# Products with v and logits in 32-column tiles, the bits of a pair moved beside them

## The chip, the cores and the metric

The kernel runs on one core of a Trainium2 chip. The metric is the device time of one execution, in microseconds (us). The engines are PE (matrix products; its weight loads have rows of their own, PEld), DVE (vector), ACT (activations and copies), POOL (elementwise here), and SP, which issues nearly all DMAs.

## What is computed

Thirty-two attention heads (4 batches of 8, sequence 768, head size 64) in which a query sees only keys of its own hash bucket, then a soft mixture of experts over the result:

```python
q_bits = (np.einsum('bhsd,dk->bhsk', q, proj) > 0)        # k_bits alike
mask = q_bucket[:, :, :, None] == k_bucket[:, :, None, :]
scores = np.where(mask, scale * q @ k.T, -1e9)
attn = np.exp(scores - scores.max(-1)); attn /= attn.sum(-1) + 1e-9
x = (attn @ v) as [3072, 512]
logits = x @ phi                     # 32 slots
slot_input = softmax(logits, 0).T @ x
slot_out = relu(slot_input[e] @ w1[e]) @ w2[e]   # 8 experts
out = softmax(logits, 1) @ slot_out
```

## The kernel before

Heads go in pairs; a pair shares one load of q and k (`raw`, two tiles of 384 KB, one buffer each). Every step is a small function (`bits`, `smax`, `scores`, `exps`, `av`, `pair_sum` and so on). The order of the program is written out by hand: each step gets a place, a number in slots (a head has 6 slots, a pair 12), from the tables `WHEN` (relative to the head's or the pair's start, repeated for all), `FIRST` (first heads) and `LAST` (last heads); `at` collects the steps, `plan.sort` orders them, and each engine executes its own instructions in that order. So a place says what stands before what on an engine, not a time.

Per head, `smax` forms masked products (128-wide tiles, stationary operand 128 columns wide) of which DVE takes row maxima (`most`), `shift` and `shift_rows` put these into the operands, `scores` forms the final products in PSUM tiles `st` (3 buffers), ACT takes the exponentials (`exps`, into `pt`), POOL adds them up (`acc`), and `av` multiplies them with v: for each of 6 key blocks, two products with a stationary operand of 64 columns, one into partitions 0 to 63 of a PSUM tile and one into 64 to 127. Six such steps stand close together. The even head's six stand at 12m + 7.3 to 7.8 (m numbers the pairs), the odd head's at 12m + 11.4 to 11.9.

Per pair, `pair_sum` adds the columns of `acc` with a stationary operand of 32 columns in four tiles side by side, `pair_log` forms the logits with a 64-column operand in two tiles, `pair_rec`, `pair_add`, `pair_turn` and `pair_x` normalise and transpose. `bits` forms the hash projections of a pair with a 32-column operand in four tiles, and DVE turns them into signed bits at once (`over`, into `bt`, one buffer), from which `spread_bits` moves rows into the operands of both heads by DMA. The sums and logits of pair m stand beside the even head's products of pair m + 1; the bits of pair m + 2 stand alone at 12m + 9.77, among 128-wide products. `split_hi` (two ACT casts) and `split_lo` (DVE) split `raw`.

The PSUM pool `p_mi` (tiles `mi`, two buffers) serves, in turn, the sums, the logits, `shift`, the bits, `pair_turn` and `pair_x`. Products of plain fp32 stand in the trace as two records for each call, that is two passes over the moving operand.

The expert weights are 64 pieces of 512 KB. 22 buffers (`wa`) are filled while attention runs, 5 more (`wb`) at slot 178, when the pool `pp` (raw, w4, bt) is freed, the others as further pools are freed; the experts' products (lines 1250 and 1304, operands of 32 columns in four tiles) end the kernel.

Of the kernel before, what the change touches and what calls it, by code (L numbers as in the profile page):

```python
# [35 lines left out]
N_WA, N_WB, N_WX, N_WY, N_WP, N_WL, N_WQ, N_WC = 22, 5, 3, 3, 4, 4, 3, 1  # L36
# [9 lines left out]
WHEN = {'load': -22.2619,  # L46
 'bits': -14.2349,
 'split_hi': -13.1979,
 'split_lo': [-12.6935, -11.1565],
 'spread': [[-13.1488, -10.4354, -5.4444, -6.6523], [-12.5668, -12.3196, -12.1201, -12.1119]],  # L50
 'load_v': [-3.3718, -2.7975],
 'smax': [[-9.1416, -8.9962, -8.5159, -6.9351, -7.288, -7.9448, -7.6967, -6.8281, -5.1392, -5.8132, -5.3072, -5.9654], [-9.427, -9.0393, -8.9496, -8.0893, -6.5956, -5.4862, -5.2511, -6.7187, -5.9555, -4.4901, -4.4112, -4.8313]],
 'scores': [[1.2975, 4.5102, 4.6485, 0.1975, 0.9854, 3.1771, 3.9797, 1.6303, 4.9362, 3.6592, 4.7491, 2.6803], [0.1022, 0.1134, 0.2578, -0.7876, 2.5023, -0.0474, -0.0019, 0.9469, 3.5414, 3.836, 4.3557, 2.1267]],
 'shift': [-3.9548, -2.943],
 'shift_rows': [-3.1833, -2.5735],
 'acc': [[5.8167, 7.9352, 8.671, 8.9926, 9.4278], [3.2448, 5.9632, 7.775, 7.9389, 9.119]],
 'av': [[7.3359, 7.3407, 7.3716, 7.6009, 7.6538, 7.8216], [5.4279, 5.6255, 5.6962, 5.7798, 5.8356, 5.8843]],
 'pair_sum': 19.3148,
 'pair_turn': 22.5366,
 'pair_rec': [19.5377, 20.5566, 20.2507],  # L60
 'pair_log': 20.0405,
 'pair_x': [22.7561, 23.3606],
 'pair_add': 20.646,
 'batch_both': 22.6105,
 'batch_max': 23.0026,
 'batch_exp': 24.3365,
 'batch_turn': 28.9128,
 'batch_scale': 25.2342,
 'batch_slots': 31.0753,
 'batch_weigh': 30.6347,  # L70
 'batch_share': 31.0459,
 'batch_arrange': 31.5634,
 'load_weights': 19.2952,
 'most': [[-8.9336, -8.4993, -6.5106, -7.0012, -7.2304, -6.107, -4.4997, -4.045, -5.7193], [-9.2445, -8.5848, -7.9972, -6.5189, -4.7861, -6.6917, -4.8511, -3.3259, -3.4925]],
 'exps': [[2.4996, 4.6616, 1.3422, 1.7274, 4.1008, 2.657, 5.6835, 5.3516, 2.8997], [0.4665, 0.6159, -0.1385, 3.5659, 1.9029, 1.0907, 3.8797, 4.6698, 2.4268]]}

FIRST = {('bits', 0): -79.2532,
 ('first_x', 0): -21.5961,
 ('first_x', 1): -38.3467,
 ('first_x', 2): -14.0186,  # L80
 ('first_x', 3): -18.1728,
 ('load', 4, 0): -11.7737,
 ('load', 4, 1): -2.4487,
 ('bits', 2): -14.1697,
 ('split_hi', 2): -6.2964,
 ('split_lo', 2, 0): -6.0272,
 ('split_lo', 2, 1): -2.7126,
 ('spread_y', 2): -1.2972,
 ('spread_bits', 2): -10.7536,
 ('spread_l', 2): -0.8689,  # L90
 ('spread_x', 2): 1.8345,
 ('smax', 1, 0, 0): -15.417,
 ('smax', 1, 0, 1): -10.3075,
 ('smax', 1, 1, 0): -8.5553,
 ('smax', 1, 1, 1): -13.1999,
 ('smax', 1, 2, 0): -7.7817,
 ('smax', 1, 2, 1): -3.054,
 ('smax', 1, 3, 0): -2.9369,
 ('smax', 1, 3, 1): -6.0953,
# [3 lines left out]
 ('smax', 1, 5, 1): -12.1189,  # L103
 ('first_y', 1): -50.9549,
# [4 lines left out]
 ('bits_rest',): -35.6422,  # L109
 ('bits_copy', 0): -76.9767,  # L110
 ('bits_copy', 1): -74.0135,
 ('first_w', 0, 0): -52.4417,
 ('first_w', 0, 1): -39.9607,
 ('copy_ident',): -29.6374,
 ('bits_out',): -11.9627,
 ('shift_first', 0): -19.0897,
 ('rows_first', 0): -18.172,
# [5 lines left out]
 ('most', 1, 4): -3.6817,  # L123
# [4 lines left out]
 ('most', 1, 11): -11.3295,  # L128
 ('bits_first', 1): -42.9165,
 ('split_hi', 0): -76.3743,  # L130
 ('split_lo', 0, 0): -31.1399,
 ('split_lo', 0, 1): -29.5113,
 ('spread_x', 0): -28.9558,
 ('load_v', 0): -17.5538,
 ('smax', 0, 0, 0): -47.8465,
 ('scores', 0, 0, 0): -13.1602,
 ('most', 0, 0): -31.4902,
 ('exps', 0, 0): -9.5739,
 ('smax', 0, 0, 1): -30.0548,
 ('scores', 0, 0, 1): -8.5463,  # L140
 ('smax', 0, 1, 0): -28.1934,
# [3 lines left out]
 ('smax', 0, 1, 1): -53.0109,  # L145
 ('scores', 0, 1, 1): -7.7493,
 ('most', 0, 3): -42.0509,
 ('exps', 0, 3): -6.5603,
 ('smax', 0, 2, 0): -37.8114,
 ('scores', 0, 2, 0): -10.6797,  # L150
 ('most', 0, 4): -30.2579,
 ('exps', 0, 4): -9.0316,
 ('smax', 0, 2, 1): -23.4528,
 ('scores', 0, 2, 1): -3.1498,
 ('smax', 0, 3, 0): -23.0743,
 ('scores', 0, 3, 0): -2.8625,
 ('most', 0, 6): -22.0438,
 ('exps', 0, 6): 1.1398,
 ('smax', 0, 3, 1): -25.2842,
 ('scores', 0, 3, 1): -0.4211,  # L160
 ('most', 0, 7): -23.2425,
 ('exps', 0, 7): 2.139,
 ('smax', 0, 4, 0): -17.1968,
 ('scores', 0, 4, 0): -11.14,
 ('most', 0, 8): -16.3427,
 ('exps', 0, 8): -8.0057,
 ('smax', 0, 4, 1): -21.9959,
 ('scores', 0, 4, 1): -5.8002,
# [82 lines left out]
 ('exps', 2, 6): 13.8394,
 ('smax', 2, 3, 1): 4.3584,
# [180 lines left out]
def lsh_attention_soft_moe(  # L433
# [956 lines left out]
```

## Time and profile before

| | us |
|---|---|
| median of 3 runs | 479.09 |
| lowest, highest | 478.86, 481.44 |
| the profiled execution | 479.32 |
| its span (first to last instruction) | 477.4 |
| PE busy | 465.7 (98%) |
| DVE, POOL, ACT busy | 356.8, 334.0, 272.7 |

The mean granted clock of PE was 0.995 of full speed. Start times in a timeline are exact to 0.01 us; the end of a matrix product is modelled and overlaps the next start, so prices are taken from start to start.

### The profile page before, as it was taken

How to read it: one execution, taken by the hardware profiler on the slowest of the kernel's cores; microseconds unless marked ns; L12 is line 12 of the kernel's file. 1: busy time of each engine (PE TensorE's matmuls, PEld its weight loads, DVE VectorE, ACT ScalarE, POOL GpSimd, SP SyncE). 2: the span in 40 equal slices, each digit the busy share in tenths (PEclk: the TensorE clock that was granted, in tenths of full speed). 3: DMA queues.
4: the chain of work that ended last, by engine and by line, in shares of the span. 5: the costliest groups of instructions: out<-in, count | busy, mean ns of one | idle time of the engine just before them, and what ended most of it. 6: DMA issues, size and time to landing. Idle time of an engine off the chain costs nothing.

```text
span 477.4 us, 9268 instructions
## 1 busy us (share of the span) xinstructions
PE 465.7 (98%) x3337; PEld 297.7 (62%) x3337; DVE 356.8 (75%) x657; ACT 272.7 (57%) x515; POOL 334.0 (70%) x207
## 2 busy tenths in 40 slices
PE   8999999999999999999999999999999999999993
PEld 6764657575757565657566575757575666663682
DVE  5867787879788797979797878787888965464142
ACT  5666566575767564756575665657575654423232
POOL 8489796969686799696947999696767997810000
PEclk9999999999999999999999999999999999999998
DMA  5774555757575747576665657675755176899986
GB/s 170 179 164 120 134 130 134 220 147 209 156 200 144 202 121 185 167 173 195 151 217 132 188 137 215 153 210 155 199 147 127 40 169 243 345 409 395 411 342 266
DMA packets 37664, 93.09 MB, mean 195 GB/s; under 512 B 7074, under 2 KB 13348, under 8 KB 37620
## 3 DMA queue, kind: packets, MB, share of 16 engines
q1 hardware_dynamic: 37492, 92.37, 66.4%
q8 instruction: 26, 0.43, 0.4%
q14 instruction: 18, 0.15, 0.1%
q10 hardware_dynamic: 96, 0.07, 0.1%
q0 software_dynamic: 32, 0.07, 0.0%
HBM read 52.76 MB, written 6.29 MB: 124 GB/s over the span
## 4 chain that ended last, share of the span: by engine, by line
PE 93%; DMA 3%; DVE 2%; SPq 0%; issue 0%; ACT 0%; DVEq 0%; ACTq 0%
PE st L754 29%; PE av L780 26%; PE smx L691 15%; PE qs L1304 3%; PE qh L1250 3%; PE mi L641 3%; PE mi L792 2%; PE mi L805 2%; PE mi L840 2%; DMA w<-w 2%; PE mi L825 1%; PE av L550 1%; PE mi L739 1%; DMA raw<-qk 1%; PE mi L998 1%; PE qh L1327 1%
## 5 line engine op out<-in xcount | busy, mean ns | idle before, releaser
L771 POOL TENSOR_TENSOR acc<-acc,pt 128x768 f32<-128x768 f32 x125 | 243.7, 1951 | 11.8 <-ACT pt L760 4.7
L760 ACT ACTIVATE pt<-st 128x512 f32<-128x512 f32 x288 | 164.6, 596 | 60.1 <-PE st L754 56.3
L754 PE MATMUL st<-XY 128*128 128x512 f32 (+1 forms) x768 | 179.1, 343 | 0.0
L703 DVE TENSOR_REDUCE mx<-smx 128x1 f32<-128x512 f32 x192 | 130.5, 687 | 32.1 <-PE smx L691 30.7
L754 PEld LDWEIGHTS st<-XY 128*128 128x128 f32 x768 | 124.2, 189 | 31.4 <-issue 18.3
L780 PE MATMUL av<-pt,v 128*64 128x384 f32 x768 | 132.6, 491 | 0.0
L691 PE MATMUL smx<-XY 96*128 96x256 f32 (+1 forms) x384 | 119.0, 363 | 1.5 <-DVE mx L703 1.0
L780 PEld LDWEIGHTS av<-pt,v 128*64 128x64 f32 x768 | 51.7, 136 | 69.3 <-issue 64.5
L768 POOL TENSOR_TENSOR acc<-pt 128x768 f32<-128x768 f32 x32 | 58.7, 1834 | 41.1 <-ACT pt L760 40.9
L691 PEld LDWEIGHTS smx<-XY 96*128 96x128 f32 x384 | 68.9, 190 | 26.3 <-DVE mx L703 10.7
L700 DVE TENSOR_REDUCE mx<-smx 128x2 f32<-128x512 f32 x96 | 65.2, 679 | 1.9 <-PE smx L691 0.9
L784 ACT COPY avs<-av 128x384 f32<-128x384 f32 x32 | 15.3, 479 | 83.6 <-PE av L780 83.6
L799 DVE RECIPROCAL sm<-sm 128x128 f32<-128x128 f32 x45 | 40.5, 929 | 15.6 <-ACT sm L795 15.5
L598 DVE TENSOR_TENSOR w<-raw,w 128x768 fp32r<-128x768 f32 x28 | 37.4, 1337 | 0.9 <-ACT w L594 0.5
L594 ACT CAST w<-raw 128x768 fp32r<-128x768 f32 x30 | 23.4, 829 | 0.7 <-DMA XY<-mr 0.3
L611 ACT CAST XY<-w 64x768 fp32r<-64x768 f32 x30 | 23.4, 829 | 0.0
L842 DVE TENSOR_TENSOR xq<-mi,r 128x256 f32<-128x256 f32 x45 | 17.5, 417 | 5.9 <-PE mi L840 5.5
L1304 PE MATMUL qs<-w 128*32 128x128 f32 x464 | 15.4, 274 | 0.3 <-issue 0.3
L1304 PEld LDWEIGHTS qs<-w 128*32 128x32 f32 x464 | 13.9, 110 | 2.0 <-issue 1.9
L840 PE MATMUL mi<-ident,avs 128*128 128x128 f32 x90 | 14.8, 273 | 0.0
L641 PE MATMUL mi<-raw,pb 128*32 128x384 f32 x120 | 13.8, 502 | 0.8 <-DMA raw<-qk 0.8
L1250 PE MATMUL qh<-w,siT 128*32 128x512 f32 x128 | 14.4, 594 | 0.0
(191 smaller groups left out, 325.6 us busy)
## 6 DMA issues: line engine op xcount, KB each, us to landing
w<-w SPq DMA_DIRECT2D x61, 512.0 KB
XY<-w SPq DMA_DIRECT2D x47, 384.0 KB
XY<-w SPq DMA_DIRECT2D x63, 192.0 KB
raw<-qk SPq DMA_DIRECT2D x30, 384.0 KB
v<-vt SPq DMA_DIRECT2D x32, 192.0 KB
out<-w SPq DMA_DIRECT2D x9, 512.0 KB
xq<-w SPq DMA_DIRECT2D x3, 512.0 KB
out<-w SPq DMA_DIRECT2D x6, 256.0 KB
```

Of the source, the lines that this page charges most:

```text
L598: (nc.vector if h > 2 else nc.gpsimd).tensor_tensor(out=w[:, 2 * x + 1], in0=st[h]["raw", x], in1=w[:, 2 * x], op=ALU.subtract)
L691: nc.tensor.matmul(pt[:, o:o + b - a], s["Y"][0:96, 0, t * P:(t + 1) * P], s["Y"][0:96, 1, a:b], start=True, stop=True)
L700: nc.vector.tensor_reduce(out=mx[:, n - 1:n + 1], in_=s["sm_ps", n - 1].rearrange("p (a x) -> p a x", a=2), axis=AX.X, op=ALU.max)
L703: nc.vector.reduce_max(out=mx[:, n:n + 1], in_=s["sm_ps", n], axis=AX.X)
L754: nc.tensor.matmul(pt[:, o:o + b - a], x[:, 1, i * P:(i + 1) * P], x[:, 0, a:b], start=first, stop=not first)
L760: nc.scalar.activation(s["P", n // 4][:, 512 * u:512 * u + 512], s["st_ps", n - (n % 4 == 2)], AF.Exp, scale=D ** -0.5)
L768: nc.gpsimd.tensor_tensor(out=s["acc"], in0=pr[:, 0:S], in1=pr[:, S:2 * S], op=ALU.add)
L771: eng.tensor_tensor(out=s["acc"], in0=s["acc"], in1=pr[:, a * S:(a + 1) * S], op=ALU.add)
L780: nc.tensor.matmul(s["av"][64 * c:64 * c + 64, 0:HC], s["v"][:, i, :], pr[:, o + c * HC:o + (c + 1) * HC], start=(i == 0), stop=(i == NT - 1))
L799: nc.vector.reciprocal(out=rs[:, k * P:(k + 1) * P], in_=rs[:, k * P:(k + 1) * P])
L1250: nc.tensor.matmul(ph[fh][32 * j:32 * j + 32], siT[:, k, 4 * g + j, :], wt[0, g, k, j][:, fh * 512:(fh + 1) * 512], start=(k == 0), stop=( ...
L1304: nc.tensor.matmul(pos[i][32 * j:32 * j + 32, 0:w], hTs[g][:, f, 32 * j:32 * j + 32], wt[1, x, 2 * g + f // 4, j][:, (f % 4) * HM + o:(f % ...
```

## The change

- `av` makes four products with 32-column operands in place of two with 64, into the same PSUM rows; `pair_log` likewise.
- The bits of pair m + 2 move from 12m + 9.77 to 12m + 7.08, in front of the even head's products with v; their sign step becomes a step of its own (`bits_over`, at 12m + 7.40), and `bt` gets two buffers.
- `wa` has 21 buffers and `wb` 6; the tile `halves` of the last stage is taken from `wb` instead of `wa`.
- All places are set anew.

```diff
-N_WA, N_WB, N_WX, N_WY, N_WP, N_WL, N_WQ, N_WC = 22, 5, 3, 3, 4, 4, 3, 1
+N_WA, N_WB, N_WX, N_WY, N_WP, N_WL, N_WQ, N_WC = 21, 6, 3, 3, 4, 4, 3, 1
...
- 'bits': -14.2349,
+ 'bits': -16.9197,
+ 'bits_over': -16.6042,
...
- 'av': [[7.3359, 7.3407, 7.3716, 7.6009, 7.6538, 7.8216], [5.4279, 5.6255, 5.6962, 5.7798, 5.8356, 5.8843]],
+ 'av': [[7.1625, 7.3716, 7.5845, 7.6308, 7.8325, 7.9673], [5.4369, 5.5215, 5.7534, 5.7926, 5.8443, 5.9134]],
  'pair_sum': 19.3148,
...
- 'pair_log': 20.0405,
+ 'pair_log': 19.6449,
...
@@ bits
-        bt = pts[3][:, 2 * P:2 * P + HC].bitcast(F32R) if h == 0 else pp.tile([P, HC], F32R, name="bt", bufs=1)
+        bt = pts[3][:, 2 * P:2 * P + HC].bitcast(F32R) if h == 0 else pp.tile([P, HC], F32R, name="bt", bufs=2)
...
         else:
-            over(bt, pts_b[0], slice(0, P))
+            st[h]["pj"] = pts_b[0]
+
+    def bits_over(h):
+        over(st[h]["bt"], st[h]["pj"], slice(0, P))
@@ av
         for c in range(2):
-            nc.tensor.matmul(s["av"][64 * c:64 * c + 64, 0:HC], s["v"][:, i, :],
-                             pr[:, o + c * HC:o + (c + 1) * HC], start=(i == 0), stop=(i == NT - 1))
+            for e in range(0, D, 32):
+                nc.tensor.matmul(s["av"][64 * c + e:64 * c + e + 32, 0:HC], s["v"][:, i, e:e + 32],
+                                 pr[:, o + c * HC:o + (c + 1) * HC], start=(i == 0), stop=(i == NT - 1))
@@ pair_log
         for a in range(2):
-            nc.tensor.matmul(pt[64 * a:64 * a + 64, 0:HC], phs[:, 2 * g + a].rearrange("p c s -> p (c s)"),
-                             st[h + a]["avs"], start=True, stop=True)
+            for c in range(2):
+                r = 64 * a + 32 * c
+                nc.tensor.matmul(pt[r:r + 32, 0:HC], phs[:, 2 * g + a, c], st[h + a]["avs"], start=True, stop=True)
@@ the plan
             at(s0 + WHEN["bits"], bits, h)
+            if h > 2:
+                at(s0 + WHEN["bits_over"], bits_over, h)
...
-    halves = piece().bitcast(F32R)
+    halves = wb.tile([P, F], F32, name="w").bitcast(F32R)
```

Sorted by the new places, the even head's stretch of a pair reads on PE: bits of pair m + 2, `av` 0, sums of pair m - 1, `av` 1 to 3, logits of pair m - 1, `av` 4 and 5. After it stand 15 steps of 128-wide tiles, then the odd head's six `av`, then 38 steps of 128-wide tiles.

## Rows read from the trace of the kernel before

**Rows 1.** The page, part 1: busy time of each engine, share, instructions.

```profile
PE 465.7 (98%) x3337; PEld 297.7 (62%) x3337; DVE 356.8 (75%) x657; ACT 272.7 (57%) x515; POOL 334.0 (70%) x207
```

**Rows 2.** The page, part 4: the chain that ended last, by engine.

```profile
PE 93%; DMA 3%; DVE 2%; SPq 0%; issue 0%; ACT 0%; DVEq 0%; ACTq 0%
```

**Rows 3.** Groups by form, PE: line, tiles, stationary and moving shape, count, busy us.

```profile
L780 PE MATMUL av<-pt,v 128*64 128x384 f32 x768 | 132.6, 491 | 0.0
L792 PE MATMUL mi<-acc,ones 128*32 128x384 f32 x120 | 12.7, 496 | 0.0
```

**Rows 4.** Timeline of PE, 206 to 232 us: start, length, instruction, count.

```profile
206.39 0.85 PE L792 MATMUL mi<-acc,ones 128*32 128x384 f32 x8
207.18 4.09 PE L780 MATMUL av<-pt,v 128*64 128x384 f32 x24
211.09 0.82 PE L805 MATMUL mi<-avs,phs 128*64 128x384 f32 x4
211.84 1.19 PE L754 MATMUL st<-XY 128*128 128x512 f32 x4
...
213.45 0.63 PE L754 MATMUL st<-XY 128*128 128x512 f32 x2
214.01 0.85 PE L641 MATMUL mi<-raw,pb 128*32 128x384 f32 x8
214.79 0.50 PE L754 MATMUL st<-XY 128*128 128x256 f32 x2
...
217.15 4.09 PE L780 MATMUL av<-pt,v 128*64 128x384 f32 x24
221.17 0.50 PE L691 MATMUL smx<-XY 96*128 96x512 f32 x1
221.51 0.63 PE L754 MATMUL st<-XY 128*128 128x512 f32 x2
221.97 0.28 PE L691 MATMUL smx<-XY 96*128 96x256 f32 x1
...
231.29 0.85 PE L792 MATMUL mi<-acc,ones 128*32 128x384 f32 x8
```

**Rows 5.** Timeline of weight loads, products with v: first and last of ten passes.

```profile
207.55 0.14 PEld L780 LDWEIGHTS av<-pt,v 128*64 128x64 f32 x2 [0.18 <-issue]
...
210.45 0.14 PEld L780 LDWEIGHTS av<-pt,v 128*64 128x64 f32 x2 [0.18 <-issue]
```

**Rows 6.** Timeline of weight loads, line 1250, four tiles: first and last of eight passes.

```profile
433.58 0.13 PEld L1250 LDWEIGHTS qh<-w,siT 128*32 128x32 f32 x4 [0.30 <-issue]
...
436.59 0.13 PEld L1250 LDWEIGHTS qh<-w,siT 128*32 128x32 f32 x4 [0.30 <-issue]
```

**Rows 7.** Timeline of SP, 219 us: issue of a pair's raw tiles.

```profile
218.99 2.74 SPq L487 DMA_DIRECT2D raw<-qk  x2
```

**Rows 8.** Stretches: length, busy of PE, PEld, DVE, ACT, POOL; PEclk; DMA share, GB/s.

```profile
206.39:212.00 5.61, 5.61 (x38) 2.24 (x38) 4.04 (x9) 1.86 (x4) 5.48 (x4) 1.00 0.60 147
...
225.00:227.00 2.00, 2.00 (x18) 1.87 (x17) 1.98 (x4) 1.47 (x4) 0.00 (x0) 1.00 0.03 8
...
400.00:405.00 5.00, 5.00 (x37) 3.58 (x37) 2.58 (x6) 3.76 (x8) 1.92 (x3) 1.00 0.58 229
```

**Rows 9.** Timeline of DVE: reciprocals; last maximum before the sums; sign of the bits.

```profile
210.04 1.75 DVE L799 RECIPROCAL sm<-sm 128x128 f32<-128x128 f32 x2
...
230.92 0.69 DVE L703 TENSOR_REDUCE mx<-smx 128x1 f32<-128x512 f32 x1 [0.71 <-PE smx L691]
...
239.84 0.68 DVE L634 TENSOR_SCALAR bt<-mi,con 128x384 fp32r<-128x384 f32 x1 [0.34 <-DMA XY<-w]
```

**Rows 10.** Timeline of ACT ahead of the odd head's products with v.

```profile
215.87 0.60 ACT L760 ACTIVATE pt<-st 128x512 f32<-128x512 f32 x1 [1.15 <-PE st L754]
216.36 1.56 ACT L594 CAST w<-raw 128x768 fp32r<-128x768 f32 x2
```

**Rows 11.** Timeline of PE: `one_rec` between the last head's products with v.

```profile
417.76 0.82 PE L867 MATMUL mi<-ident,r 128*64 128x128 f32 x12
```

More of the change, by code (lines that the diff above doesn't have):

```diff
@@ L77 @@
-FIRST = {('bits', 0): -79.2532,
- ('first_x', 0): -21.5961,
[L79 to L85, printed above, removed]
+WHEN = {'load': -21.9936,
+ 'bits': -16.9197,
+ 'bits_over': -16.6042,
+ 'split_hi': -13.2983,
+ 'split_lo': [-12.9149, -11.0826],
+ 'spread': [[-12.0915, -11.5469, -8.953, -6.655], [-12.3785, -12.3512, -12.3006, -12.3201]],
+ 'load_v': [-3.517, -2.7904],
+ 'smax': [[-9.1583, -8.8492, -8.5159, -6.9351, -7.288, -7.7897, -7.668, -6.6324, -5.8421, -5.3545, -5.3072, -6.0549], [-9.7632, -9.0445, -8.8249, -8.0893, -7.1228, -5.4744, -5.2243, -6.7941, -5.9373, -3.923, -3.8073, -4.8117]],
+ 'scores': [[1.2693, 4.5102, 4.6471, 0.6549, 1.1749, 3.4157, 4.0851, 2.3161, 5.0574, 3.6729, 4.936, 2.8195], [0.1022, 0.1305, 0.2578, -0.3502, 2.5023, -0.152, -0.1357, 0.8237, 2.7131, 3.3028, 3.9913, 2.1129]],
+ 'shift': [-4.2829, -2.8223],
+ 'shift_rows': [-3.9493, -2.5735],
+ 'acc': [[6.578, 8.483, 8.7628, 9.3376, 9.8127], [3.5552, 6.8688, 7.7213, 8.3507, 9.1163]],
+ 'av': [[7.1625, 7.3716, 7.5845, 7.6308, 7.8325, 7.9673], [5.4369, 5.5215, 5.7534, 5.7926, 5.8443, 5.9134]],
+ 'pair_sum': 19.3148,
+ 'pair_turn': 22.7192,
+ 'pair_rec': [20.4835, 20.4184, 20.4906],
+ 'pair_log': 19.6449,
+ 'pair_x': [22.7561, 23.3975],
+ 'pair_add': 20.6395,
+ 'batch_both': 22.629,
+ 'batch_max': 24.0715,
+ 'batch_exp': 25.6339,
+ 'batch_turn': 29.2014,
+ 'batch_scale': 28.697,
+ 'batch_slots': 30.8526,
+ 'batch_weigh': 30.7496,
+ 'batch_share': 31.5307,
+ 'batch_arrange': 31.6666,
+ 'load_weights': 18.0049,
+ 'most': [[-8.5075, -8.3842, -6.6454, -6.844, -7.465, -6.0513, -4.5809, -4.4336, -5.9589], [-8.5428, -8.3256, -7.9972, -5.0984, -4.6541, -6.7765, -4.7712, -3.123, -3.8464]],
+ 'exps': [[2.3226, 4.7089, 1.5866, 1.6189, 4.1904, 2.8646, 5.3978, 5.0219, 3.3233], [0.4665, 0.8469, -0.0665, 4.9993, 1.8447, 0.9966, 3.5184, 4.708, 2.4182]]}
@@ L86 @@
+FIRST = {('bits', 0): -78.9437,
+ ('first_x', 0): -21.5961,
+ ('first_x', 1): -38.4577,
+ ('first_x', 2): -17.2679,
+ ('first_x', 3): -19.2525,
+ ('load', 4, 0): -11.7197,
+ ('load', 4, 1): -1.8445,
+ ('bits', 2): -14.1163,
+ ('split_hi', 2): -7.1223,
  ('split_lo', 2, 0): -6.0272,
- ('split_lo', 2, 1): -2.7126,
+ ('split_lo', 2, 1): -2.7078,
  ('spread_y', 2): -1.2972,
- ('spread_bits', 2): -10.7536,
- ('spread_l', 2): -0.8689,
- ('spread_x', 2): 1.8345,
+ ('spread_bits', 2): -11.2012,
+ ('spread_l', 2): -1.5808,
+ ('spread_x', 2): 1.9596,
@@ L122 @@
  ('most', 1, 3): -12.0749,
- ('most', 1, 4): -3.6817,
+ ('most', 1, 4): -3.581,
  ('most', 1, 6): -2.3199,
@@ L373 @@
  ('smax', -1, 2, 1): -13.3913,
- ('scores', -1, 2, 1): -3.2707,
- ('smax', -1, 3, 0): -13.0844,
+ ('scores', -1, 2, 1): -4.2487,
+ ('smax', -1, 3, 0): -13.1507,
  ('scores', -1, 3, 0): -3.039,
- ('most', -1, 6): -12.2557,
+ ('most', -1, 6): -11.9934,
  ('exps', -1, 6): -2.8946,
@@ L380 @@
  ('scores', -1, 3, 1): -3.5376,
- ('most', -1, 7): -12.8688,
- ('exps', -1, 7): -1.0328,
- ('smax', -1, 4, 0): -10.127,
- ('scores', -1, 4, 0): -5.4497,
- ('most', -1, 8): -9.9172,
- ('exps', -1, 8): -4.5502,
+ ('most', -1, 7): -12.6457,
+ ('exps', -1, 7): -1.6771,
+ ('smax', -1, 4, 0): -10.2955,
+ ('scores', -1, 4, 0): -5.7287,
+ ('most', -1, 8): -10.0396,
+ ('exps', -1, 8): -4.6761,
  ('smax', -1, 4, 1): -10.9638,
@@ L392 @@
  ('exps', -1, 10): -2.7193,
- ('smax', -1, 5, 1): -12.0887,
+ ('smax', -1, 5, 1): -12.0289,
  ('scores', -1, 5, 1): -2.6723,
- ('most', -1, 11): -11.7487,
+ ('most', -1, 11): -11.5741,
  ('exps', -1, 11): -0.987,
- ('shift', -1): -8.279,
+ ('shift', -1): -8.9168,
  ('shift_rows', -1): -7.6557}
```

326 lines of the change are left out of this document (150 added, 176 removed).

## The prediction

> **What bounds the kernel now.** I read the page's engine shares first: PE is busy 98% of the span, the next engine 75% [rows 1]. The chain that ended last is PE for 93% [rows 2]. A busy PE need not be a fast one, so I went on to the timeline of one pair (it repeats every 24.90 us, from the sums at 206.39 to those at 231.29 [rows 4]) and read start to start where PE loses time between products that stand back to back. The reader is to see there that nothing waits for another engine, but that each change of tile width costs a fixed bit [rows 4].
>
> *Inside one width.* A pass of a product with v (384 columns, two tiles of 64) takes (210.45 - 207.55) / 9 = 0.322 us, and its loads are hidden [rows 5]. A pass with four tiles of 32 takes (436.59 - 433.58) / 7 = 0.430 us for 512 columns [rows 6]. Both are 0.84 ns a column: four narrow tiles stream as fast as two wide ones.
>
> *Between widths.* A call has two passes, 0.645 us. The logits, same width as the products before them, take 0.75 to the next 128-wide start: 0.105 more, the emptying of the array [rows 4]. The sums take 0.79 to the first product with v: 0.145 more, which is 0.10 of the same kind and 0.04 for starting a narrow stretch (its first load cannot be hidden, and four tiles start one after the other). The six products with v after them take 3.91 for 12 passes that are worth 3.87: 0.045 for the first load of 64 columns. Going into the bits: two 512-column products at 0.23 each (221.51 to 221.97 is two) would end at 213.91, the bits start at 214.01: 0.10. Coming back to 128 columns: 221.17 to 221.51 is 0.34 for a product worth 0.23, 0.11 for its first load [rows 4].
>
> **The change part by part.**
>
> *Bits.* Alone among 128-wide products they cost 0.10 (in) + 0.78 (214.01 to 214.79) + 0.11 (first load behind) = 0.99 us of PE [rows 4]. In the stretch of sums and products with v, all of 32 columns now, they cost their two passes, 0.645.
>
> *Sums, products with v, logits.* Before: 206.39 to 211.84, 5.45 us [rows 4]. After, with the bits: 9 calls or 18 passes at 0.322 = 5.80, plus 0.04 at the start and 0.105 at the end, 5.95. So a pair pays 0.50 more there and 0.99 less at the old place: **-0.49 us**.
>
> *The odd head's stretch* takes 4.02 [rows 4]; in narrow tiles 12 x 0.322 + 0.04 + 0.105 = 4.01. Nothing, -0.01.
>
> *Count.* There are 15 groups of sums in the loop (120 records, eight in each) [rows 3], and 14 of bits behind the first two. Sorting the new places, 13 groups of bits (heads 6 to 30) share a stretch with sums: 13 x 0.49 = 6.4. The sums of heads 26 and 28 have no bits beside them and save the change alone, 2 x 0.135 = 0.3. Some 20 stretches of `av` alone save 0.01, together 0.2. Against it: the bits of head 4, which stood behind an `av`, now stand alone, one excursion more, +0.25; and in the last head `one_rec` stays 64 wide between narrow products, where it was the same width [rows 11]: two changes for the first (0.10 + 0.045 and 0.10 + 0.04), one for the second (0.145), +0.4. Sum: -6.4 - 0.3 - 0.2 + 0.25 + 0.4 = **-6.2 us**. The profiled execution took 479.32 (its span is 477.4), which gives 473.1; it lies 0.2 above the median of 479.09, and there I forecast **472.9 us**.
>
> *What the moved steps rest on.* (1) The bits read `raw` 2.7 slots earlier. Its two tiles are issued at 218.99 to 221.73 [rows 7]; after 225 the DMA engines are at 0.03 [rows 8]; the new place is the start of the next such stretch, 231.29 [rows 4]. Six us of cover; the load's own place moves by 0.3 slots, half a us. With the cover gone PE, and all behind the bits, would wait for the landing. (2) `bits_over` is a DVE step of 0.68, and DVE is free 0.3 us after the stretch starts (230.92 + 0.69) [rows 9]. It waits there for the bits, and `most` and `shift` queue behind it. PE needs it at the logits, which take the same `mi` buffer and come after six calls, 3.9 us; the bits are there after about 0.9, their sign after 1.6. Nothing. (3) On DVE the sign, two maxima, `shift`, three reciprocals at 0.87 [rows 9] and `pair_add` now stand in this order ahead of the odd head's first maximum. The old stretch held 4.04 us of them, with 0.3 of an earlier maximum [rows 8]; with the sign (0.68), a second maximum (0.69), `pair_add` (two steps of 384 columns, an estimate of 1.1 from the sign's 0.68) and the 0.9 before the bits are there, DVE comes to that first maximum at 7.1 and ends it at 7.8 us after the stretch starts. The ninth 128-wide step, which needs the PSUM tile that it reads, is reached at 5.95 + 2.2. Cover 0.35: I cost it at nothing, at most one maximum, 0.69. (4) ACT's two casts of `split_hi`, 1.56 us [rows 10], now stand ahead of the exponentials of two key blocks of the odd head, which its third and fifth `av` read. I lay the 128-wide steps at 0.23 and 0.12: from the end of the stretch PE reaches the odd head's `av` 2 after about 5.6 us, and ACT (copy, row, two exponentials, casts, two more at 0.60) ends the last of them at about 5.3. Cover: 0.3 us, thin. Behind this wait stands the rest of that stretch. (5) On SP the order changes little; a piece of weights less in the loop and one more at slot 178 is 512 KB, 1.3 us at 229 / 0.58 = 395 GB/s, in a time in which the DMA engines have room (0.58) [rows 8]. `halves` takes a buffer whose weights were used before. Nothing.
>
> *What no row shows.* Products with v in four tiles don't exist yet. Lower bound: the pitch of row group 6, no loss. Upper: the sums' own 384-column passes, (0.79 - 0.10) / 2 = 0.345, 0.023 more each [rows 4]. I take the lower: the sums never get past their first call, line 1250 runs on as the products with v will. Also unknown is the order of 128-wide steps among themselves (transposes beside long products): between -0.1 and +0.1 a pair, that is -1.5 to +1.5 us; I take 0.
>
> *A rule against it.* Four loads of a pass start within 0.02 us of each other, 0.007 apart [rows 6], and the question is whether that offset is paid at every pass. The Trainium skill, TensorE: Matmul & The Clock Gate, section "Measured speedup vs the span model", has a packed group last one product plus about 4 ns for each further tile; if that held for every pass, two tiles more would cost 8 ns x 414 passes = 3.3 us as an estimate, and the time would be 476.2. The trace speaks against it: at 0.84 ns a column in both groups the offset is paid once a stretch [rows 5, 6].
>
> **The rivals.**
>
> *Offset at each pass.* The row's 0.007 for each of two more tiles on 32 x 12 + 15 x 2 = 414 passes is 5.8 us, and eats the gain: 478.7. For it: more instructions a pass. Against: the equal pitch. The same result, about 479, would come if PE emptied between lines as well as between widths; but from the first product with v to the logits 12 passes took 3.91, no 0.10 over their worth and the first load [rows 4]. Together 7%.
>
> *Half the gain, 476.* Waits of about 0.25 us a pair from point (3) or (4), or narrow passes 0.007 dearer. For it: the two thin covers. Against: no such wait now. 8%.
>
> *Slower.* One mechanism: the casts ahead of the exponentials. If PE reaches the odd head's products earlier than I lay it, or `raw` or w4 is late for the casts, `av` 2 waits for ACT. From 0.48 us a pair on it eats all. If the cover is gone and all 1.56 us show but 0.3, a pair costs 1.26 - 0.49 = 0.77 more, 13 of them 10 us: 489. For it: ACT's order. Against: ACT is busy 57% [rows 1]. 6%.
>
> **How the numbers follow.** Forecast 79%, half 8%, none 7%, slower 6%. The forecast's own spread is 471 to 474.5 (order of the 128-wide steps, 0.6 us for the start and the end). The range 470.8 to 476.2 takes in half the gain and leaves out the last two rivals and a little on each side. About 0.5%, 2.4 us, is what a measurement can tell from no change: faster 86%, same 8%, slower 6%.
>
> **What would show it.** The timeline of a pair: bits, six `av`, sums, logits without a gap, 5.95 us long; no bits alone among 128-wide products; the odd head's stretch 4.01; a period of 24.4 in place of 24.90. Wrong it would be if passes with v were over 0.335 apart, if an `av` waited for ACT's `pt`, or if the logits waited for `bt`.

## The result, and the profile after

| | before | after |
|---|---|---|
| median, us | 480.26 (4 runs, beside the changed kernel) | 474.97 (4 runs) |
| lowest to highest | 478.86 to 481.58 | 474.43 to 475.23 |
| ratio, 95% interval | | 0.989 (0.985 to 0.993) |
| span of the profiled execution | 477.39 | 473.37 |

The changed kernel is 5.3 us faster by the medians and 4.0 by the two profiled spans. In the runs beside the experiments before had medians of 479.59 to 479.84 (66 runs together); against these the gain is 4.6 to 4.9. The forecast was 472.9, 6.2 less than before, with a range of 470.8 to 476.2: the time is in the range, 2.1 above the forecast.

The page of the changed kernel, part 1 (busy time of each engine) and part 4 (the chain that ended last), the lines that answer to [rows 1, 2]:

```profile
PE 460.5 (97%) x4165; PEld 297.3 (63%) x4165; DVE 348.7 (74%) x657; ACT 270.3 (57%) x515; POOL 331.3 (70%) x207
...
PE 87%; DVE 3%; DMA 2%; ACT 2%; SPq 1%; issue 1%; POOL 1%; DVEq 0%; ACTq 0%; POOLq 0%
```

PE still sets the time, with 828 more product records in 5 us less of busy time. The last line says already that the path leaves PE a little more often than it did.

The timeline of PE in a pair of the changed kernel, which answers to [rows 4]:

```profile
203.18 0.85 PE L642 MATMUL mi<-raw,pb 128*32 128x384 f32 x8
203.85 0.83 PE L785 MATMUL av<-pt,v 128*32 128x384 f32 x8
204.50 0.83 PE L797 MATMUL mi<-acc,ones 128*32 128x384 f32 x8
205.14 2.12 PE L785 MATMUL av<-pt,v 128*32 128x384 f32 x24
207.07 0.83 PE L812 MATMUL mi<-avs,phs 128*32 128x384 f32 x8
207.72 1.47 PE L785 MATMUL av<-pt,v 128*32 128x384 f32 x16
209.12 0.30 PE L743 MATMUL mi<-ident,mz 128*72 128x128 f32 x1
...
213.39 4.08 PE L785 MATMUL av<-pt,v 128*32 128x384 f32 x48
217.40 0.62 PE L695 MATMUL smx<-XY 96*128 96x512 f32 x2
...
227.56 0.85 PE L642 MATMUL mi<-raw,pb 128*32 128x384 f32 x8
```

The reader is to see one stretch from the bits at 203.18 to the next 128-wide product at 209.12: 5.94 us, where 5.95 was worked out. The odd head's stretch is 213.39 to 217.40, 4.01, as worked out. Three products with v take 205.14 to 207.07, 1.93 for six passes, 0.322 each, the lower bound of the prediction. From bits to bits a plain pair takes 24.38 in place of 24.90: 0.52 won, 0.49 forecast.

Where the lead was won and lost can be read at one event that both kernels have in the same place, the first product with v of an odd head. In us ahead of before: head 1, none; 3, 1.05; 9, 2.61; 11, 2.57; 17, 4.27; 19, 4.41; 25, 6.10; 27, 6.20; 29, 6.51; 31, 5.98; first product of the experts, 5.57; last product of PE, 4.83; end of the span, 4.02. So plain pairs give about 0.5, the three in which the end of a batch is worked off (up to heads 11, 19 and 27) give -0.04, 0.14 and 0.10, and 2.5 us go back behind head 29. The first pair (head 1 to 3) gives 1.10, more than its two parts are worth: 0.55 of it is a wait for a maximum that shrank, 0.97 at 46.32 in before and 0.42 at 45.80 here.

**The batch ends.** Two waits stand there that plain pairs don't have. PE and ACT of the changed kernel, first in the odd head's stretch at the end of the first batch, then among the scores at the end of the second (an idle time and what ended it stand in brackets):

```profile
138.52 1.15 PE L785 MATMUL av<-pt,v 128*32 128x384 f32 x12
139.87 1.50 PE L785 MATMUL av<-pt,v 128*32 128x384 f32 x16 [0.20 <-ACT pt L764]
```

```profile
136.51 0.51 ACT L909 COPY dl<-lacc 64x384 f32<-64x384 f32 x1
137.27 1.57 ACT L595 CAST w<-raw 128x768 fp32r<-128x768 f32 x2 [0.25 <-DMA XY<-w]
138.74 1.08 ACT L764 ACTIVATE pt<-st 128x512 f32<-128x512 f32 x2
...
244.35 0.62 ACT L932 ACTIVATE dl<-dl,run_n 64x384 f32<-64x384 f32 x1
244.98 0.20 ACT L932 ACTIVATION_READ_ACCUMULATOR dl<-dl,run_n 64x1 f32 x1
245.09 0.28 ACT L934 ACTIVATE al<-run_n,run_n 64x1 f32<-64x1 f32 x1
245.28 1.54 ACT L764 ACTIVATE pt<-st 128x512 f32<-128x512 f32 x3
```

```profile
245.90 0.30 PEld L758 LDWEIGHTS st<-XY 128*128 128x128 f32 x2 [0.36 <-ACT pt L764]
```

The first is the thin cover of point (4): `batch_both`'s copy (L909, 0.51) stands ahead of the casts, which start 0.91 ahead of this stretch (138.18) in place of 1.46 in a plain pair, the exponential ends later, and the product with v waits. In the second `batch_exp` (L932, L934), 0.93 from its start to the next exponential, stands among exponentials, and the scores wait for an `st` tile. The prediction cost neither.

**The end.** In the experts' products PE stands still and waits for nothing that the profile shows. (A standstill is given here from start to start, less 0.12 us, about what a pass of four records takes in this row; the chain's "issue" shows less, since the end of a product is modelled.) The chain of the changed kernel there:

```profile
450.96 1.95 PE qs L1312 x63
452.91 0.66 PE qh L1335 x3
454.51 1.75 PE qs L1312 x57
456.26 0.72 issue
456.98 2.17 PE qs L1312 x71
```

Before has one such standstill, 0.49 at 453.21; here there are two, 0.23 at 450.96 and 0.87 at 456.98. Last, SP takes 4.08 us in place of 3.08 over the issue of the last six output transfers in this execution; no run was made for that, and the profiles of e7 and e11 below have 3.33 and 3.24.

### The profile page after: what moved, and what is told of

The parts are those of the page before. It is cut to its first block, busy times and chain, and to the rows that moved or that the text cites. A ratio compares the mean times of both kernels' runs of the same rounds, so it can differ in the third digit from the quotient of the medians.

```text
span 473.4 us, 10927 instructions
## 1 busy us (share of the span) xinstructions
PE 460.5 (97%) x4165; PEld 297.3 (63%) x4165; DVE 348.7 (74%) x657; ACT 270.3 (57%) x515; POOL 331.3 (70%) x207
## 4 chain that ended last, share of the span: by engine, by line
PE 87%; DVE 3%; DMA 2%; ACT 2%; SPq 1%; issue 1%; POOL 1%; DVEq 0%; ACTq 0%; POOLq 0%
PE st L758 26%; PE av L785 24%; PE smx L695 14%; PE qs L1312 3%; PE qh L1258 3%; PE mi L642 2%; PE mi L812 2%; PE mi L797 2%; PE mi L846 2%; SPq L603 1%; PE mi L743 1%; PE av L551 1%; DMA XY<-w 1%; POOL acc L775 1%; PE mi L1004 1%
## 5 line engine op out<-in xcount | busy, mean ns | idle before, releaser
L775 POOL TENSOR_TENSOR acc<-acc,pt 128x768 f32<-128x768 f32 x125 | 238.8, 1911 | 34.0 <-ACT pt L764 26.9
L785 PE MATMUL av<-pt,v 128*32 128x384 f32 x1536 | 137.7, 488 | 0.4 <-ACT pt L764 0.2
L758 PEld LDWEIGHTS st<-XY 128*128 128x128 f32 x768 | 126.0, 190 | 18.0 <-ACT pt L764 2.6
L695 PE MATMUL smx<-XY 96*128 96x256 f32 (+1 forms) x384 | 117.5, 358 | 0.9 <-DVE mx L707 0.4
L785 PEld LDWEIGHTS av<-pt,v 128*32 128x32 f32 x1536 | 46.9, 110 | 70.3 <-issue 64.6
L772 POOL TENSOR_TENSOR acc<-pt 128x768 f32<-128x768 f32 x32 | 60.8, 1901 | 15.5 <-ACT pt L764 15.5
L804 DVE RECIPROCAL sm<-sm 128x128 f32<-128x128 f32 x45 | 38.5, 911 | 2.9 <-ACT sm L800 2.9
L599 DVE TENSOR_TENSOR w<-raw,w 128x768 fp32r<-128x768 f32 x28 | 32.6, 1166 | 0.7 <-POOL acc L775 0.7
L635 DVE TENSOR_SCALAR bt<-mi,con 128x384 fp32r<-128x384 f32 x15 | 10.1, 676 | 21.4 <-PE mi L642 21.4
L800 ACT ACTIVATE sm<-mi,eps 128x384 f32<-128x384 f32 x15 | 8.7, 581 | 23.8 <-PE mi L797 23.8
```

The lines of the kernel that those rows point to most:

```text
L599: (nc.vector if h > 2 else nc.gpsimd).tensor_tensor(out=w[:, 2 * x + 1], in0=st[h]["raw", x], in1=w[:, 2 * x], op=ALU.subtract)
L695: nc.tensor.matmul(pt[:, o:o + b - a], s["Y"][0:96, 0, t * P:(t + 1) * P], s["Y"][0:96, 1, a:b], start=True, stop=True)
L758: nc.tensor.matmul(pt[:, o:o + b - a], x[:, 1, i * P:(i + 1) * P], x[:, 0, a:b], start=first, stop=not first)
L772: nc.gpsimd.tensor_tensor(out=s["acc"], in0=pr[:, 0:S], in1=pr[:, S:2 * S], op=ALU.add)
L775: eng.tensor_tensor(out=s["acc"], in0=s["acc"], in1=pr[:, a * S:(a + 1) * S], op=ALU.add)
L785: nc.tensor.matmul(s["av"][64 * c + e:64 * c + e + 32, 0:HC], s["v"][:, i, e:e + 32], pr[:, o + c * HC:o + (c + 1) * HC], start=(i == 0), ...
```

## The experiments

Four questions: is each part worth its price by itself, do the places matter, what do they matter for, and what makes PE stand still at the end. Times are medians, ratios those to before from the same chip, and a plain period is sums to sums in a pair without a batch end.

### Each part alone, and both at the old places

`e1_bits_alone`: before, with the bits beside the sums (and what they need: `bits_over`, two `bt`, 21 + 6 pieces), products with v and logits still 64 wide.

```diff
- 'bits': -14.2349,
+ 'bits': -16.7,
+ 'bits_over': -16.6042,
-N_WA, N_WB, N_WX, ... = 22, 5, 3, ...
+N_WA, N_WB, N_WX, ... = 21, 6, 3, ...
```

> Kernel before with one part: the bits of the pair two ahead moved in front of the sums (place 12m + 7.30, sign step at 12m + 7.40, two buffers for bt, 21 + 6 pieces); products with v and logits stay 64 columns wide, all other places as before. Widths theory (each change of tile width costs 0.10 us plus the first load): 97 stretches of one width in place of 122, -0.35 us for each of 13 pairs, +0.25 for head 4: -4.2 us against the kernel before. Rival (the gain of the change comes from the new order of the other steps): within 1 us of before.

Measured: 480.97, ratio 1.0031 (1.0019 to 1.0043), plain period 24.97 to 25.00 (24.58 right behind a batch end). No gain. PE now waits for DVE's maxima, by 0.3 to 0.6 us from start to start, in every pair but those right behind a batch end; the longest is at the first batch's end, at 147.15:

```profile
147.15 0.50 PE L695 MATMUL smx<-XY 96*128 96x512 f32 x1 [0.39 <-DVE mx L707]
```

`e2_narrow_alone`: before, with the products with v and the logits in tiles of 32.

```diff
-            nc.tensor.matmul(s["av"][64 * c:64 * c + 64, 0:HC], s["v"][:, i, :], ...)
+            for e in range(0, D, 32):
+                nc.tensor.matmul(s["av"][64 * c + e:64 * c + e + 32, 0:HC], s["v"][:, i, e:e + 32], ...)
```

> Kernel before with the other part alone: products with v and logits in 32-column tiles, bits at their old place, all places as before. Widths theory: the change between sums and products with v goes (0.135 us in 15 pairs), two more changes around one_rec at the end: -1.8 to -2.3 us. Rival that narrow passes are dearer (0.345 in place of 0.322 us): +7 us. Rival that the places make the gain: 0.

Measured: 479.57, ratio 0.9986 (0.9967 to 1.0005). The plain period is 24.75, 0.15 less as priced, and the lead on before grows by 0.95 from head 1 to 17 and by 0.60 from 19 to 31; but PE's standstills at the end come to 1.4 us in place of 0.5, and between the two stretches the scores lose 1.1 at 253.80 (0.94 of it put down to the transfer of shift's row).

`e3_both_old_places`: both parts, every other place as before. So the diff is that of e1 and e2 together.

> Both parts of the change, but all other places as in the kernel before (bits at 12m + 7.30). Widths theory: -6.2 us against before if nothing waits; the changed kernel has -0.5 us per pair in plain pairs but loses 0.4 us in each of three pairs at a batch's end, where its new places put batch_exp behind two exponentials and the casts ahead of an exponential that an av needs. If those places are the loss, this kernel is 1 to 1.5 us faster than the changed one; if the new places are worth something elsewhere, it is slower than the changed one.

Measured: 480.46, ratio 1.0015 (1.0003 to 1.0026), plain period 24.81 in the mean of nine, pairs with a batch end 26.96 to 27.59. **Both parts at the old places gain nothing.** What the changed kernel wins needs the places too, which the prediction had at zero. (The new places without the two parts were not run.) What is late is again a maximum, by 0.3 to 0.6 a pair from start to start, and DVE's timeline says why. First POOL, then DVE of e3:

```profile
214.41 8.74 POOL L775 TENSOR_TENSOR acc<-acc,pt 128x768 f32<-128x768 f32 x4 [1.02 <-ACT pt L764]
...
216.31 1.84 POOL L775 TENSOR_TENSOR acc<-acc,pt 128x768 f32<-128x768 f32 x1
...
218.23 2.42 POOL L775 TENSOR_TENSOR acc<-acc,pt 128x768 f32<-128x768 f32 x1
...
216.38 2.58 DVE L599 TENSOR_TENSOR w<-raw,w 128x768 fp32r<-128x768 f32 x1
218.89 0.68 DVE L707 TENSOR_REDUCE mx<-smx 128x1 f32<-128x512 f32 x1
```

and the same steps of the changed kernel:

```profile
214.63 8.18 POOL L775 TENSOR_TENSOR acc<-acc,pt 128x768 f32<-128x768 f32 x4 [4.15 <-ACT pt L764]
...
213.49 0.95 DVE L599 TENSOR_TENSOR w<-raw,w 128x768 fp32r<-128x768 f32 x1
214.36 0.68 DVE L707 TENSOR_REDUCE mx<-smx 128x1 f32<-128x512 f32 x1
```

One and the same step, `split_lo`, takes 0.95 us while POOL is idle and 2.58 beside POOL's running sums: it starts at 216.38, 0.07 behind the start of a step of POOL that ends at 216.31 + 1.84 = 218.15, and ends 0.81 after that; POOL's next step starts at 218.23 and takes 2.42 in place of 1.84. Each waits for the other. The Trainium skill, SBUF — State Buffer, section "Who interferes with whom", has the rule: "A DVE instruction with two SBUF inputs contends with a GpSimd instruction that reads SBUF". The traces agree, with 1.6 us for DVE and 0.6 for POOL. In two of e3's nine plain pairs, those of 25.13 and 25.14, `split_lo` also starts late: at 192.58 it had waited 1.25 us for ACT's casts. So the order on ACT has a part in e3's loss.

### Is it the running sums?

`e8_sums_short`: e3, with the odd heads' running sums on POOL cut to their first step. It leaves out the rest of those sums, so the softmax of odd heads isn't normalised as in the reference; its time (2 runs) is that of a kernel with less work on POOL.

```diff
-            if n:
+            if n and not (x and n > 1 and h < BH - 1):
                 at(s0 + WHEN["acc"][x][n - 1], acc, h, n)
```

> Kernel e3 with POOL's sums of the odd heads cut to their first step (blocks 2 to 5 are left out of the sums, except in the last head, so the result is not the reference's). Contention theory: split_lo takes 0.95 us each time, the period of a plain pair is 24.4 us, about 5 us faster than e3. Rival (order on DVE): period stays at 24.8.

Measured: 475.41, ratio 0.9911 (0.9884 to 0.9938), 5.05 us less than e3; eight of nine plain periods are 24.39 to 24.44. At the old places, without the sums beside it, the price of the widths comes out in full. Before with its sums cut was not run; but behind the first pair its products with 128-wide tiles wait nowhere in the loop for a maximum, so the cut had little to give there.

`e12_rec_behind`: e3, with the reciprocals behind the maxima and the logits one slot earlier, the order in which DVE has them in the changed kernel.

```diff
- 'pair_rec': [19.5377, 20.5566, 20.2507],
- 'pair_log': 20.0405,
+ 'pair_rec': [20.4835, 20.4184, 20.4906],
+ 'pair_log': 19.6449,
```

> Both parts at the old places (e3_both_old_places), and only the three reciprocals and the logits at the new places: all reciprocals behind the two maxima and the shift on DVE, the logits one slot earlier. Theory A, split_lo beside POOL's running sums (2.58 us at 216.38 in e3, 0.95 in the changed kernel) makes the maxima late: nothing in that is touched, split_lo's mean stays at 1450 to 1550 ns, the plain period at 24.8, time 479.5 to 481. Theory B, the order of the reciprocals is what the new places bring: the plain period falls to 24.4 to 24.6, time 475 to 477.5.

Measured: 480.81, ratio 1.0015 (1.0001 to 1.0028), plain period 24.82 in the mean of nine. So that order isn't what the new places bring. One plain pair of e12 is as short as in the changed kernel, 24.40, with all of POOL's sums in place. There `split_lo` starts only 0.16 before a step of POOL ends, and it takes 0.98. First POOL, then DVE:

```profile
292.29 1.84 POOL L775 TENSOR_TENSOR acc<-acc,pt 128x768 f32<-128x768 f32 x1
...
293.97 0.98 DVE L599 TENSOR_TENSOR w<-raw,w 128x768 fp32r<-128x768 f32 x1
```

So what counts in this pair is not how much POOL works, but where in a step of POOL `split_lo` starts. The groups of `split_lo` on DVE (busy us, mean ns) of e3, e12, e8 and the changed kernel:

```profile
L599 DVE TENSOR_TENSOR w<-raw,w 128x768 fp32r<-128x768 f32 x28 | 42.2, 1506 | 4.7 <-ACT w L595 3.9 <-DMA v<-vt 0.5
```

```profile
L599 DVE TENSOR_TENSOR w<-raw,w 128x768 fp32r<-128x768 f32 x28 | 41.2, 1471 | 3.8 <-ACT w L595 2.4 <-DMA v<-vt 1.1
```

```profile
L599 DVE TENSOR_TENSOR w<-raw,w 128x768 fp32r<-128x768 f32 x28 | 29.2, 1043 | 4.4 <-ACT w L595 3.0 <-DMA v<-vt 1.2
```

```profile
L599 DVE TENSOR_TENSOR w<-raw,w 128x768 fp32r<-128x768 f32 x28 | 32.6, 1166 | 0.7 <-POOL acc L775 0.7
```

The first two kernels gain nothing, the last two do. Before has 1337 for it: it pays a part of this price too, in a pair 0.5 us longer, where the maxima hardly came late for it (PE waited 1.0 us for them in the whole run, by the page, 0.97 of it in the first pair).

### The logits

`e4_logits_wide`: the changed kernel, with the logits 64 wide again.

```diff
-            for c in range(2):
-                r = 64 * a + 32 * c
-                nc.tensor.matmul(pt[r:r + 32, 0:HC], phs[:, 2 * g + a, c], st[h + a]["avs"], ...)
+            nc.tensor.matmul(pt[64 * a:64 * a + 64, 0:HC], phs[:, 2 * g + a].rearrange("p c s -> p (c s)"), ...)
```

> Changed kernel with the logits back in two 64-column tiles, in the middle of the narrow stretch: two changes of width more in each of 15 pairs, 0.10 + 0.045 and 0.10 + 0.04 us each. Widths theory: +4.3 us against the changed kernel (to about -1 us against before). Rival (order, not width): no difference to the changed kernel.

Measured: 479.04, 4.1 us above the changed kernel; ratio to before 0.9984 (0.9975 to 0.9993). The plain period is 24.69, 0.31 more, where 0.285 was expected; two of the nine plain pairs take 25.24 and 25.42, with a wait for the transfer of shift's row. The stretch of e4:

```profile
207.00 2.12 PE L785 MATMUL av<-pt,v 128*32 128x384 f32 x24
209.05 0.87 PE L810 MATMUL mi<-avs,phs 128*64 128x384 f32 x4
209.84 0.53 PE L785 MATMUL av<-pt,v 128*32 128x384 f32 x4
```

The same three calls with v take 2.05 to the logits in place of 1.93, and the logits 0.79 in place of 0.65: 0.12 going out of the width, 0.14 coming back. The price of a change of width holds between 32 and 64 columns too, and this kernel with one 64-wide call in the stretch has lost three quarters of the gain, a part of it to the two waits for shift's row.

### The casts ahead of the exponentials

In the new order the odd head's exponential of two key blocks stands behind `split_hi`'s casts, which was the prediction's mechanism for slower. Three runs move it.

`e5_casts_first`: e3, with the new place of that exponential.

```diff
- 'split_hi': -13.1979,
+ 'split_hi': -13.2983,
- 'exps': [..., [0.4665, 0.6159, -0.1385, 3.5659, ...
+ 'exps': [..., [0.4665, 0.6159, -0.1385, 4.9993, ...
```

> Kernel e3 (both parts of the change, old places) with one order changed on ACT: the two casts of split_hi ahead of the exponential of the odd head's third block, as in the changed kernel. That exponential starts POOL's next sums, so POOL is idle while DVE subtracts (split_lo). Contention theory (split_lo takes 0.95 us alone and up to 2.6 us beside POOL's sums, and in e3 PE then waits for DVE): first split_lo 0.95 us in place of 2.58, the period of a plain pair 24.4 us in place of 24.84, 4 to 6 us faster than e3. Rival (the other new places on DVE make the difference): within 1 us of e3.

Measured: 501.91, ratio 1.0473 (1.0444 to 1.0502), 21 us slower than e3. At the old places 4.9993 is also behind `spread_y`'s two casts, which the new places have later. The group of the products with v in e5 (its last part is idle time before them):

```profile
L785 PE MATMUL av<-pt,v 128*32 128x384 f32 x1536 | 136.2, 493 | 21.2 <-ACT pt L764 21.1 <-ACT avs L789 0.2
```

`e10_casts_first2`: the same with 4.80, behind `split_hi`'s casts and ahead of `spread_y`'s.

```diff
+ 'exps': [..., [0.4665, 0.6159, -0.1385, 4.80, ...
```

> Both parts at the old places (e3_both_old_places), and one step moved: the odd head's exponential that held up split_hi's casts, from place 3.57 to 4.80, which is behind split_hi's two casts but still ahead of spread_y's (e5_casts_first had put it behind both). Theory A, the contention of POOL's running sums with split_lo on DVE: later exponentials give later sums on POOL, split_lo (mean 1506 ns in e3) comes down to about 1200, the maxima are on time and the plain period falls from 24.8 to about 24.4; time 475 to 477, 3.5 to 5 us under e3. Theory B, the order of the reciprocals and maxima on DVE alone is what the new places bring: split_lo may fall, the smax stay late, period 24.7 to 24.8, time within 1.5 us of e3 (479 to 481). Theory C, the thin cover: PE waits for ACT's exponential at the odd head's products with v, 0.2 us or more a pair, time 482 or more.

Measured: 481.51, ratio 1.0038 (1.0022 to 1.0054). `split_lo` comes down to 1279 ns and no plain pair waits for a maximum any more, as theory A has it; three of the nine plain periods are 24.48 to 24.50. But the others are 24.57 to 25.72: in four of these six PE waits 0.21 to 1.04 for ACT, theory C, and in one (25.35) 0.40 for the transfer of shift's row. ACT, then PE in a pair of 24.94:

```profile
217.55 1.57 ACT L595 CAST w<-raw 128x768 fp32r<-128x768 f32 x2 [0.33 <-DMA XY<-w]
219.02 0.59 ACT L764 ACTIVATE pt<-st 128x512 f32<-128x512 f32 x1
...
217.91 1.50 PE L785 MATMUL av<-pt,v 128*32 128x384 f32 x16
219.66 2.79 PE L785 MATMUL av<-pt,v 128*32 128x384 f32 x32 [0.26 <-ACT pt L764]
```

The casts start 0.36 ahead of the odd head's products. In the changed kernel they start 1.46 ahead of those products (213.39), and the exponential ends in time:

```profile
211.93 1.57 ACT L595 CAST w<-raw 128x768 fp32r<-128x768 f32 x2 [0.23 <-DMA XY<-w]
```

That is the cover of point (4): with 1.46 it holds in plain pairs, with 0.36 it doesn't. Which of the many new places brings the casts forward was not tried.

`e6_exps_first`: the changed kernel with the old order, exponential ahead of the casts.

```diff
- 'exps': [..., [0.4665, 0.8469, -0.0665, 4.9993, ...
+ 'exps': [..., [0.4665, 0.8469, -0.0665, 3.5659, ...
```

> Changed kernel with the one order undone: the exponential of the odd head's third block ahead of the casts again (place 12m + 9.57). Contention theory: POOL's sums start earlier, the first split_lo runs beside them and takes 1.6 to 2.6 us, PE waits for DVE: 2 to 6 us slower than the changed kernel. Cover theory of the prediction (casts ahead of that exponential only endanger the product with v behind it): the wait of 0.16 us in batch pairs goes, 0.5 us faster.

Measured: 476.51, ratio 0.9936 (0.9918 to 0.9954), 1.5 us above the changed kernel by the medians and 2.3 by the two ratios. `split_lo` is at 1434 ns again, but only two plain pairs lose by it (24.80 and 24.81), those in which one takes 2.63; where it takes 1.5, the others' 24.33 to 24.34 show no loss. Pairs with a batch end take 26.80 to 26.84: one `split_lo` takes 2.1 to 2.2 there, and PE waits 0.68 for a maximum. The range expected of the contention, 2 to 6 us, was missed from below or just met: this order is a part of what the new places bring, not all of it. And the mean of `split_lo` alone doesn't tell the loss; the long ones do.

### A better version

`e7_batch_early`: the changed kernel with `batch_max` and `batch_exp` earlier, so that the exponential of the logits no longer stands among those of the scores.

```diff
- 'batch_max': 24.0715,
- 'batch_exp': 25.6339,
+ 'batch_max': 23.0026,
+ 'batch_exp': 24.3365,
```

> Changed kernel with batch_max and batch_exp at the places of the kernel before (batch_exp right behind the copy of avs, not between exponentials). In the trace of the changed kernel scores wait about 0.3 us for ACT in each of three pairs at a batch's end: 0.8 us faster if that is the cause; 0 if ACT is late anyway.

Measured: **473.59** (473.29 to 474.46), ratio 0.9876 (0.9859 to 0.9894), 1.4 us less than the changed kernel's median (0.6 by the two ratios). Pairs with a batch end take 26.08 to 26.10 in place of 26.36 to 26.43. ACT of e7 where the change had `batch_exp` among the exponentials:

```profile
242.05 0.62 ACT L932 ACTIVATE dl<-dl,run_n 64x384 f32<-64x384 f32 x1
...
242.97 2.64 ACT L764 ACTIVATE pt<-st 128x512 f32<-128x512 f32 x5
```

Three pairs by 0.3 make 0.9, the lower end of what was expected. But five of the nine plain pairs take 24.46 to 24.68 in this trace, 0.85 more together, in bits too small to be placed, and the loop as a whole is no shorter than the changed kernel's; the 1.6 us between the two spans lie in the start (0.6) and behind the first product of the experts (1.0). So e7 has the lower median, its mechanism shows at its place, and the 1.4 us aren't shown to be its doing; the intervals of the two ratios overlap.

`e11_one_narrow`: e7, with `one_rec`, `one_fold` and `one_log` in tiles of 32 as well.

```diff
-                nc.tensor.matmul(pt[64 * c:64 * c + 64, k * P:(k + 1) * P], ...broadcast_to([P, D]), ident, ...)
+                nc.tensor.matmul(pt[32 * c:32 * c + 32, k * P:(k + 1) * P], ...broadcast_to([P, 32]), ident, ...)
```

> The kernel with batch_max and batch_exp early (e7_batch_early) and, in the last pair, one_rec, one_fold and one_log in tiles of 32 columns too, so that no width changes between the products there. By the price of a change (0.10 of drain and 0.04 of a first load, two changes for the first head, one for the second, and one at each one_log): 0.4 to 0.7 us less than e7_batch_early, 472.9 to 473.2. If the lead lost in the tail (6.2 us ahead at 370, 5.6 ahead at 418) had another cause than the widths, no gain: 473.6.

Measured: 473.94, ratio 0.9876 (0.9861 to 0.9891): the same as e7. The trace has the gain at its place: from the last sums to the first product of the experts 26.65 in place of 27.09, 0.44. From there to the end it has 47.64 in place of 46.99, 0.65 more, of which 0.4 are longer standstills of PE.

### What makes PE stand still

`e9_fetch_phase`: the changed kernel with 16 more idle products ahead of everything.

```diff
-    keep_warm(7, True)
+    keep_warm(23, True)
```

> The changed kernel with 16 more idle products ahead of the first one (23 in place of 7), which moves every later instruction of PE 32 instructions on in its instruction stream and nothing else. Theory A, PE stands still because the next 16 KB packet of its instructions came too late: the two standstills of the last stage (0.23 at 450.96 and 0.87 us at 456.98, 2.6 and 2.3 us behind the start of such a packet) move to other products, about 32 instructions earlier in the work, and change in length; stalls may appear in the loop. Theory B, the weights of those very products land late: the standstills stay at the same products with the same lengths, 0.2 and 0.9 us. Time by A between 474 and 476, by B 475.

Measured: 479.65, ratio 0.9991 (0.9975 to 1.0007). The time, 4.7 above the changed kernel, is of little use: the idle products hold up the first maxima by 2.6 us, in the profiled execution one batch end takes 1.0 more (PE waits 0.72 for ACT at 342.43), and the rest is not accounted for. The place of the standstills is what counts. Each fp32 product has two records, so all later ones move by 32. The chain of e9 at the end:

```profile
452.81 1.10 PE qs L1312 x33
454.00 2.83 PE qs L1312 x95
...
458.44 0.88 PE qs L1312 x25
459.32 0.88 issue
460.20 3.04 PE qs L1312 x103
```

In the changed kernel the second one stands behind 57 products of its group of 128, here behind 25: 32 earlier in the work, and so at the same point of PE's stream, about the 3990th record. In e11, which has 30 more records ahead, it stands behind 27. Theory B (weights that land late for those very products) falls, and the fixed place in the stream is what theory A asks for. The instruction queue's part of the page for two stretches of 1 and 0.5 us of the changed kernel, from 448 and from 454.5:

```profile
q8 instruction: 1, 0.02, 6.7%
```

```profile
q8 instruction: 1, 0.02, 12.4%
```

Each has one packet (0.54 MB in 33 packets is 16 KB); the two standstills end 2.6 and 2.3 us after these packets start. The whole run has 33 of them in place of 26, for 4165 records in place of 3337. That PE waits for such a packet is argued from this and not shown: 6.7% of 1 us and 12.4% of 0.5 us on 16 engines make 1.1 and 1.0 us of transfer, so the transfers had ended 1.5 and 1.3 us before PE went on. What sets the length of a standstill was not tried.

## Why the prediction was right

**The prices.** Bits -0.49 a pair: -0.52. The stretch 5.95: 5.94; the odd head's 4.01: 4.01; a narrow pass 0.322: 0.322, no loss by more tiles, so the first rival falls, and with it the packed group's offset for every pass, by which the time would have been 476.2; the trace speaks against that use of the rule of the Trainium skill, TensorE: Matmul & The Clock Gate, section "Measured speedup vs the span model". At head 29 the lead is 6.51; the sum without `one_rec` is 6.65. That they meet so closely is luck: the three pairs with a batch end gave 1.3 less than priced, and the first pair and the nine plain ones together 1.1 more, 0.55 of it the wait in the first pair that the prediction didn't count.

**Point (1), (2), (5)** held: no product waits for `raw`, `bt` or a piece of weights that didn't before. **Point (3)** held by its numbers: the first maximum behind `pair_add` runs from 210.31 to 210.99, which is 7.1 to 7.8 after the bits, as worked out. **Point (4)** is the step whose cover was thin, and it is: it holds in plain pairs, `batch_both`'s copy of 0.51 breaks it behind a batch end, and e10 shows what a pair costs without it. The rival that ended slower was real: with the exponential behind all four casts at the old places e5 took 501.91.

**What the sum lacked.** (a) The places were costed at zero, as an order of 128-wide steps worth 1.5 us either way. They are worth the whole gain: without them both parts give 480.46. The step that failed is the count of `split_lo`'s duration as fixed. The trace of before had it (one `split_lo` of 1.62 us and one of 1.04 in a pair), and the prediction looked at DVE's order but not at what POOL does beside it. The time came out all the same because the new places take care of it, and the prediction gave no reason why they would: in this it was right by luck. (b) Pairs with a batch end were priced like plain ones: about 0.4 less gain in each of three, 1.3 us, of which e7 has 0.9 back in those pairs. (c) Behind head 29, 0.94 were lost up to the experts where `one_rec` was priced at 0.4; e11 wins 0.44 back, so the price was right, and of the rest 0.2 is a wait of `shift_rows` for DVE at 396.93, which before doesn't have. (d) Standstills of PE at the end, 1.1 in place of 0.5, were not foreseen. The number of packets is not their cause: e1, with 26 packets and 3337 records like before, stands still for 1.4 (0.5 at 454.77, 0.9 at 460.95). The 0.8 between the last product and the end stand in this one profile; by the medians the kernel won 5.3 of the 6.2.

What stays open: which of the other places bring the casts forward, what the new places would do without the two parts, what makes PE stand still at fixed points of its stream and for how long, and why scores wait, at a few places of e2, e3, e4, e8, e10 and e12, 0.3 to 1.0 us for the transfer of shift's row.

## What to carry to other kernels

Count the changes of tile width on PE, not the products: each cost 0.10 to 0.14 us between the widths of 32, 64 and 128 columns here, so calls of one width belong in one stretch and the last call of another width is the one to convert. When a bound engine gets faster, check every step of the others that had room only because of the old period, and look at what runs beside it: a step's duration from one trace holds only for what stood beside it there. A step moved across another queue's step is a change in its own right; price the pairs that differ from the plain one (a batch end, the last head) one by one.

## What the runs showed of the hardware

Two things had not been expected. `split_lo` on DVE and a running sum on POOL, both with two operands in SBUF, don't share but block each other: `split_lo` takes 0.95 us alone and up to 2.63 (e6) beside a sum, POOL's step 2.42 in place of 1.84, and where `split_lo` starts as a step of POOL ends it takes 0.98 (e12). And in a long row of short products (the experts', line 1312, a pass of four records in 0.11 us) PE stood still for 0.1 to 1.3 us at fixed points of its stream, 128 records apart, 2.2 to 2.6 us behind the start of a 16 KB packet of its instruction queue. That it ran out of instructions there is likely, and not shown.
